# Attention scores as couples of 64-row matmuls, in one stage, without stacking copies

## The chip, the cores and the metric

The kernel runs on one core of a Trainium2 chip. Its engines work side by side: TensorE does the matmuls (PE in the rows; PEld is its weight loader), VectorE (DVE) and ScalarE (ACT) the elementwise work, GpSimd (POOL) a little at the start, and SyncE's queue (SP) issues the DMAs. The metric is the device time of one execution in microseconds (us); lower is better.

## The reference

Attention with a sliding window of 128 positions and 4 sink positions, then a feed-forward layer (FFN). Shapes: `q`, `k`, `v` are [4, 8, 768, 64] (batch, heads, positions, width), `w_in` is [512, 2048], `w_out` [2048, 512], all float32.

```python
scores = np.matmul(q, k.transpose(0, 1, 3, 2)) / np.sqrt(D)
keep = (pos[None, :] < n_sink) | ((rel >= 0) & (rel < window))   # rel = pos[:, None] - pos[None, :]
scores = np.where(keep, scores, -1e9); scores -= scores.max(-1, keepdims=True)
a = np.exp(scores); a /= a.sum(-1, keepdims=True) + 1e-9
x = np.matmul(a, v)                     # [B, H, S, D] -> [B*S, H*D] = [3072, 512]
h = x @ w_in
out = (h * np.clip(h + 3, 0, 6) / 6) @ w_out
```

## The kernel before

A unit is 256 positions (two tiles of 128, called t) of one batch: 4 batches x 3 units make 12 units. Attention is done by pairs of heads: 4 pairs for a unit, 48 in all (list `pus`; the four units at the start of a sequence come first). A head has 64 channels, so one pair fills the 128 partitions with K, Q or V: head 0 in rows 0 to 63, head 1 in rows 64 to 127.

Nearly all matmuls use fp32r operands, split into a rounded high part and the remainder as a low part (`split_parts`, `copy_r`: a copy on ACT, a subtraction on DVE). The first 12 pairs are "plain" (`plain`): their scores are plain fp32 matmuls of 64 rows, straight from the loaded `kr` and `qr` (L334). The other 36 are "split". For them `B_k` and `B_q` make `kt` and `qt` (high, low), and eight SP DMAs stack these into `K` and `Q`, where one head's channels fill all 128 rows: Q high over Q low, K high twice, K low twice. One full-height matmul (L338) with Q as weights then gives two of the four products of parts; two matmuls make the scores of one head and tile. A split pair so has 8 score matmuls, and for the 32 split pairs that are not at the start of a sequence they have 272 columns (128 previous, 128 own, 16 sink positions).

Then for each pair: `C_mask` (DVE, L355: score plus mask, and its minimum), `merge` (DVE L363), `C_exp` (ACT L382), `C_sum` (DVE), `C_norm` (ACT L369), `C_sinks` (the sink columns `ssc`, DVE), `D_pt` (PE transposes, L419 and L421), `D_part` (triangles of the transposed blocks, `pm`, DVE L436), `D_out` (`ph` on ACT, `pl` on DVE), `D_sinks` (`pz`, ACT L459), `E_av` (products with V, PE L495), `E_low`/`E_sum`/`E_split` (`tmp`, `xh`, `xl`). `A_split` splits V.

The FFN of a finished unit is a queue of 32 steps for PE: `ffn1` (12 matmuls of 256 columns into one `hps`, L554) and `ffn2` (6 of 512 columns into an output bank `o`, L581). Two `ffn1` and two `ffn2` alternate. Each finished `hps` posts `activate` (`gf`: ACT, then DVE) one tick later and `split` (`gh`, then `g` on DVE) two ticks later. `drain(1)` emits one step.

From slot 14 on the order of PE, ACT, DVE and SP is written out by hand. One slot handles one pair and runs the 8 stages of `STAGES` (L709); each ends with one drained FFN step, so a slot has 8 steps and a unit's 4 slots its 32. Within a slot `s` the steps speak of three pairs: loads and splits of K and Q for pair s, scores to transposes for pair s-1, products with V for pair s-2. `F` puts the posted work in. Engines work their own instructions in order. PSUM has 8 banks, all one pool (`bank`); a new tile waits until the old one's readers are done. `kt`, `qt`, `K` and `Q` have one buffer each.

Of the kernel before, what the change touches and what calls it, by code (L numbers as in the profile page):

```python
# [9 lines left out]
F32 = mybir.dt.float32  # L10
# [8 lines left out]
P = 128  # L19
# [25 lines left out]
def attn_ffn_kernel(ctx: ExitStack, tc: tile.TileContext, qx, kx, vx, vfx, vsx, n_sink, window, w_in, w_out, out):  # L45
# [210 lines left out]
        if not planned:  # L256
            A_split(s)

    def A_split(s):
        split_parts(nc, *st_[s]["vr"], nc.scalar, nc.vector)  # L260

    def B_k(s, part=None):
        if plain(s):
            return
        w = ncol(pus[s][1])
        d = st_[s]
        if part != 1:
            d["kt"] = work.tile([P, 2, 400], F32R, name="kt", bufs=1)  # L270
            copy_r(nc, nc.scalar, d["kt"][:, 0, 0:w], d["kr"][:, 0:w])
        if part == 0:
            return
        kt = d["kt"]
        nc.vector.tensor_tensor(out=kt[:, 1, 0:w], in0=d["kr"][:, 0:w], in1=kt[:, 0, 0:w].bitcast(F32), op=ALU.subtract)
        K = work.tile([P, 2, 2, 400], F32R, name="K", bufs=1)
        for h in range(2):
            for r in range(2):
                nc.sync.dma_start(out=K[D * r:D * (r + 1), h, :, 0:w].bitcast(F32),
                                  in_=kt[D * h:D * (h + 1), :, 0:w].bitcast(F32))  # L280
        d["K"] = K

    def B_q(s, part=None):
        if plain(s):
            return
        d = st_[s]
# [7 lines left out]
        Q = work.tile([P, 2, UT], F32R, name="Q", bufs=1)  # L294
        for h in range(2):
            for r in range(2):
                nc.sync.dma_start(out=Q[D * r:D * (r + 1), h, :].bitcast(F32),
                                  in_=qt[D * h:D * (h + 1), r, :].bitcast(F32))
        d["Q"] = Q

    def spans(u):
        if u:
# [9 lines left out]
            return st_[s][f"P{h}"][:, t * P + c0:t * P + c1]  # L312
        return st_[s]["P"][:, h, t, c0:c1]

    def C_score(s, h, planned=False):

        b, u, p = pus[s]
        d = st_[s]
        if h == 0:
            d["nb"], d["sm"], d["rc"] = (work.tile([P, 4], F32, name=x, bufs=3) for x in ("nb", "sm", "rc"))  # L320
            if not plain(s):
                d["P"] = work.tile([P, 2, 2, WP], F32, name="Pt", bufs=1)
        elif plain(s):
            return
        heads = range(2) if plain(s) else (h,)
        found = []
        for t, (k0c, w, m) in enumerate(spans(u)):
            ts, ks = slice(t * P, (t + 1) * P), slice(k0c, k0c + w)
            sp = {g: ps.tile([P, 512], F32, tag="bank", name="sp") for g in heads}
            found.append(sp)  # L330
            for g in heads:
                if plain(s):
                    gs = slice(D * g, D * (g + 1))
                    nc.tensor.matmul(out=sp[g][:, 0:w], lhsT=d["qr"][gs, ts], rhs=d["kr"][gs, ks],  # L334
                                     start=True, stop=True)
                else:
                    for part in range(2):
                        nc.tensor.matmul(out=sp[g][:, 0:w], lhsT=d["Q"][:, g, ts], rhs=d["K"][:, g, part, ks],  # L338
                                         start=(part == 0), stop=(part == 1))
            if not planned:  # L340
                C_mask(s, t, sp)
        d[f"sp{h}"] = found
        if u and h == 1 and not planned:
            merge(s)

    def C_mask(s, t, sp):
        b, u, p = pus[s]
        d = st_[s]
        k0c, w, m = spans(u)[t]
        for g in sp:  # L350
# [192 lines left out]
    def ffn1(x, i, pool, psum, half, state, tag):  # L543
# [12 lines left out]
        if half == 1:  # L556
            g = pool.tile([P, 2, UT], F32R, tag="g", name="g", bufs=2)
            gh = pool.tile([P, 2, UT], F32R, tag="gh", name="gh", bufs=2)
            gf = pool.tile([P, 2, UT], F32, tag="gf", name="gf", bufs=2)
            state[i] = (gh, g)  # L560

            def activate():
                nc.scalar.activation(out=gf, in_=hp, func=AF.Relu, bias=three, scale=1.0)  # L563
                nc.vector.scalar_tensor_tensor(out=gf, in0=gf, scalar=6.0, in1=hp, op0=ALU.min, op1=ALU.mult)  # L564

            def split():
                copy_r(nc, eng(GHI, state["n"] * NP), gh, gf)
# [98 lines left out]
                queues.append(ffn_steps(units.index((b, u)), xt[(b, u)], work, ps, ps, dsts, "bank"))  # L666

    FROM = 3 * NP + 2
    ORDER = "V C0 - C1 E0 X - E1 L - N - Bk - Bq W - D0 - D1 -"
    MULT = [1] * 9 + [2] * 3  # L670
    WN = [0, 1, 1, 1, 1, 2, 2, 2, 3, 6, 6, 7]

    for s in range(FROM):
        if s == 3:
            later_constants()
        for step in ORDER.split():
            if step == "-":
                drain(MULT[s] if s < len(MULT) else 1)
            elif step in ("C0", "C1", "X", "N"):
                if 0 <= s - 1 < NS:  # L680
                    if step[0] == "C":
                        C_score(s - 1, int(step[1]))
                    else:
                        {"X": C_exp, "N": C_norm}[step](s - 1)
                    if step == "X" and s - 1 < NP:
                        keep_busy(2 * WARM[2] if s > 1 else WARM[1])
            elif step[0] == "E":
# [18 lines left out]
            elif step[0] == "D" and 0 <= s - 1 < NS:  # L706
                D_pt(s - 1, int(step[1]))

    STAGES = ("v C0 p1 F o1 z", "C1 E0 t0 F", "t1 m F a0 Kh Qh", "E1 F X Kl Ql b0", "c F N", "S F a1 b1 vs", "D0 x F V", "D1 p0 F o0 L")  # L709

    def stage(s, steps):
        c, e = s - 1, s - 2
        for step in steps.split():
            if step == "F":
                run_due()
            elif step in ("v", "Kh", "Kl", "Qh", "Ql", "V", "L", "vs"):
                if step == "L":
                    if s + 1 < NS:
                        A_kq(s + 1)
                elif s < NS and step != "vs":  # L720
                    {"v": lambda: A_v(s, True), "Kh": lambda: B_k(s, 0), "Kl": lambda: B_k(s, 1),
                     "Qh": lambda: B_q(s, 0), "Ql": lambda: B_q(s, 1), "V": lambda: A_split(s)}[step]()
                if c < NS and pus[c][1:] == (1, 0):
                    if step == "v":
                        batch_loads(pus[c][0])
                    elif step == "vs":
                        batch_split()
            elif step in ("C0", "C1", "t0", "t1", "m", "X", "c", "N", "S", "D0", "D1", "p0", "o0"):
                if c < NS:
                    {"C0": lambda: C_score(c, 0, True), "C1": lambda: C_score(c, 1, True),  # L730
                     "t0": lambda: [C_mask(c, t, st_[c]["sp0"][t]) for t in range(2)],
                     "t1": lambda: [C_mask(c, t, st_[c]["sp1"][t]) for t in range(2)],
                     "m": lambda: merge(c) if pus[c][1] else None, "X": lambda: C_exp(c, True), "c": lambda: C_sum(c),
                     "N": lambda: C_norm(c, True), "S": lambda: C_sinks(c), "D0": lambda: D_pt(c, 0, True),
                     "D1": lambda: D_pt(c, 1, True), "p0": lambda: D_part(c, 0), "o0": lambda: D_out(c, 0)}[step]()
            elif step in ("p1", "o1", "z"):
                if s > FROM and e < NS:
                    {"p1": lambda: D_part(e, 1), "o1": lambda: D_out(e, 1), "z": lambda: D_sinks(e)}[step]()
            elif e < NS:
                {"E0": lambda: slot_E(e, 0, True), "E1": lambda: slot_E(e, 1, True), "a0": lambda: E_low(e, 0),  # L740
                 "b0": lambda: E_sum(e, 0), "a1": lambda: E_low(e, 1), "b1": lambda: E_sum(e, 1),
                 "x": lambda: E_split(e)}[step]()

    ET = mybir.EngineType
    with tc.manual_schedule(engines={ET.PE, ET.Activation, ET.DVE, ET.SP}):
# [179 lines left out]
```

## Time and profile before

| | |
|---|---|
| device time, 3 runs | 726.91, 728.89, 730.55 us; median 728.89 |
| the profiled execution | 727.6 us; its span, first to last instruction, 725.7 us |
| PE busy | 708.4 us, 98% of the span |
| PE weight loads | 636.0 us, 88% |
| DVE, ACT busy | 514.6 us (71%), 449.2 us (62%) |
| granted TensorE clock, mean | 0.999 of full speed |

A timeline row gives start and duration in us, engine, line, operation and tiles; several equal instructions are merged in one row (x4), whose duration runs to the end of the last. Matmul durations hold the way through the array, so matmuls overlap in them: what one costs is the distance to the start of the next. In brackets stands how long the engine was idle before, and what ended that.

### The profile page before, as it was taken

What the parts mean: (1) busy time and instruction counts of PE and PEld (TensorE: products, weight loads), DVE (VectorE), ACT (ScalarE), POOL (GpSimd) and SP (SyncE); (2) the same over time, 40 slices, a digit from 0 to 9 for tenths busy, and PEclk for the clock granted to TensorE, in tenths of its full rate; (3) what the DMA queues carried; (4) which work ended last, traced back from release to release, by engine and by line L of the source; (5) the groups of instructions that cost most, each with busy time, mean ns of one, the idle gap of its engine ahead of it and who ended that gap; (6) DMA issues with size and microseconds to landing.
All of it is one profiled execution on the core that took longest, in us unless ns stands there. A gap on an engine that the chain in (4) does not pass through costs nothing.

```text
span 725.7 us, 13651 instructions
## 1 busy us (share of the span) xinstructions
PE 708.4 (98%) x4804; PEld 636.0 (88%) x4804; DVE 514.6 (71%) x1330; ACT 449.2 (62%) x1171; POOL 5.0 (1%) x19
## 2 busy tenths in 40 slices
PE   8999999999999999999999999999999999999996
PEld 7777887899989989988999898999998998899995
DVE  5799996446677778777877786777777877775321
ACT  5999875546447656666666566665756665654322
POOL 2000000000000000000000000000000000000000
PEclk9999999999999999999999999999999999999999
DMA  7667563124444544454345534644454454420000
GB/s 242 190 201 238 184 216 95 45 80 109 128 118 102 135 123 119 113 137 134 103 115 142 131 98 119 150 119 119 120 131 116 120 126 125 127 70 1 30 1 33
DMA packets 53549, 87.23 MB, mean 120 GB/s; under 512 B 8161, under 2 KB 36321, under 8 KB 53473
## 3 DMA queue, kind: packets, MB, share of 16 engines
q1 hardware_dynamic: 53328, 86.28, 43.1%
q8 instruction: 40, 0.66, 0.4%
q14 instruction: 37, 0.30, 0.1%
q10 hardware_dynamic: 144, 0.00, 0.0%
HBM read 42.21 MB, written 6.29 MB: 67 GB/s over the span
## 4 chain that ended last, share of the span: by engine, by line
PE 79%; ACT 10%; DVE 5%; DMA 4%; issue 2%; ACTq 0%; DVEq 0%; SPq 0%
PE hps L554 33%; PE o L581 30%; PE av L495 7%; PE sp L338 5%; PE pt L419 2%; ACT Ph L382 2%; DMA st<-in_w_out_dram 2%; ACT wt L153 1%; ACT Pt L369 1%; ACT st L157 1%; DVE pm L436 1%; ACT ph L35 1%; ACT Ph L369 1%; PE sp L334 1%; ACT pf L35 1%
## 5 line engine op out<-in xcount | busy, mean ns | idle before, releaser
L554 PE MATMUL hps<-xh,wih 128*128 128x256 f32 x768 | 221.1, 288 | 2.0 <-ACT wih L35 1.4
L554 PE MATMUL hps<-xh,wil 128*128 128x256 f32 x768 | 217.1, 283 | 0.0
L554 PE MATMUL hps<-xl,wih 128*128 128x256 f32 x768 | 216.4, 282 | 0.1
L581 PE MATMUL o<-woh,gh 128*128 128x512 f32 x384 | 153.7, 400 | 1.3 <-DVE gh L41 1.3
L581 PE MATMUL o<-woh,g 128*128 128x512 f32 x384 | 152.4, 397 | 0.1
L581 PE MATMUL o<-wol,gh 128*128 128x512 f32 x384 | 151.2, 394 | 0.0
L554 PEld LDWEIGHTS hps<-xh,wih 128*128 128x128 f32 x768 | 144.8, 189 | 4.7 <-ACT wih L35 1.7
L554 PEld LDWEIGHTS hps<-xl,wih 128*128 128x128 f32 x768 | 144.9, 189 | 1.9 <-DVE xl L517 0.3
L554 PEld LDWEIGHTS hps<-xh,wil 128*128 128x128 f32 x768 | 144.7, 188 | 0.8 <-DVE nb L355 0.7
L564 DVE SCALAR_TENSOR_TENSOR gf<-gf,hps 128x512 f32<-128x512 f32 x96 | 65.6, 684 | 72.7 <-ACT gf L563 72.7
L563 ACT ACTIVATE gf<-hps,three 128x512 f32<-128x512 f32 x96 | 65.8, 686 | 76.2 <-PE hps L554 75.9
L35 ACT ACTIVATE ph<-pm 128x512 fp32r<-128x512 f32 x64 | 40.5, 632 | 101.8 <-DVE pm L436 101.8
L581 PEld LDWEIGHTS o<-woh,g 128*128 128x128 f32 x384 | 72.1, 188 | 20.3 <-DVE g L568 3.3
L581 PEld LDWEIGHTS o<-woh,gh 128*128 128x128 f32 x384 | 72.3, 188 | 12.9 <-ACT Ph L369 1.5
L581 PEld LDWEIGHTS o<-wol,gh 128*128 128x128 f32 x384 | 72.5, 189 | 11.2 <-issue 0.3
L382 ACT ACTIVATE Pt<-Pt,nb 128x144 f32<-128x144 f32 (+2 forms) x144 | 58.6, 409 | 35.5 <-DVE Pt L363 31.8
L568 DVE TENSOR_TENSOR g<-gf,gh 128x512 fp32r<-128x512 f32 x96 | 66.2, 690 | 16.8 <-ACT gh L35 14.1
L30 DVE TENSOR_TENSOR pl<-pm,ph 128x512 fp32r<-128x512 f32 x64 | 44.3, 692 | 30.4 <-ACT ph L35 27.9
L338 PE MATMUL sp<-K,Q 128*128 128x272 f32 (+2 forms) x288 | 48.7, 291 | 2.3 <-DMA Q<-qt 1.6
L355 DVE CUSTOM_DVE_ANT_0 Pt<-sp,m_t 128x272 f32<-128x272 f32 x128 | 50.2, 434 | 0.0
L338 PEld LDWEIGHTS sp<-K,Q 128*128 128x128 f32 x288 | 42.7, 188 | 7.5 <-issue 2.0
L35 ACT ACTIVATE gh<-gf 128x512 fp32r<-128x512 f32 x72 | 44.9, 624 | 6.8 <-DVE gf L564 6.8
(99 smaller groups left out, 993.8 us busy)
## 6 DMA issues: line engine op xcount, KB each, us to landing
K<-kt SPq DMA_DIRECT2D x128, 200.0 KB, 3.3
Q<-qt SPq DMA_DIRECT2D x144, 64.0 KB, 2.4
st<-in_w_in_dram SPq DMA_DIRECT2D x16, 512.0 KB, 4.1
st<-in_w_out_dram SPq DMA_DIRECT2D x16, 512.0 KB, 4.7
kr<-in_kx_dram SPq DMA_DIRECT2D x32, 200.0 KB, 2.7
qr<-in_qx_dram SPq DMA_DIRECT2D x48, 128.0 KB, 2.4
out_dram<-ost SPq DMA_DIRECT2D x24, 256.0 KB, 2.2
vr<-in_vx_dram SPq DMA_DIRECT2D x32, 192.0 KB, 2.9
```

What stands on the lines that cost most here:

```text
L30: lo_engine.tensor_tensor(out=lo, in0=src, in1=hi.bitcast(F32), op=ALU.subtract)
L35: nc.scalar.mul(out=out, in_=src, mul=scale)
L338: nc.tensor.matmul(out=sp[g][:, 0:w], lhsT=d["Q"][:, g, ts], rhs=d["K"][:, g, part, ks], start=(part == 0), stop=(part == 1))
L355: d["min"] = nc.vector.tensor_tensor_reduce(out=cell(s, g, t, 0, w), in0=sp[g][:, 0:w], in1=m[:, 0:w], scale=-SCALE, scalar=3.0e38, op0=AL ...
L369: nc.scalar.mul(out=blk, in_=blk, mul=c)
L382: d["exp"] = nc.scalar.activation(out=blk, in_=blk, func=AF.Exp, scale=-1.0, bias=d["nb"][:, i:i + 1], accum_out=d["sm"][:, i:i + 1])
L495: nc.tensor.matmul(out=o, lhsT=l, rhs=r, start=(j == 0 and (h == 0 or not plain(s))), stop=(j == len(seq) - 1 and (h == 1 or not plain(s))))
L554: nc.tensor.matmul(out=hp[:, half, :], lhsT=l, rhs=r, start=(j == 0), stop=(j == n - 1))
L563: nc.scalar.activation(out=gf, in_=hp, func=AF.Relu, bias=three, scale=1.0)
L564: nc.vector.scalar_tensor_tensor(out=gf, in0=gf, scalar=6.0, in1=hp, op0=ALU.min, op1=ALU.mult)
L568: eng(GLO, state["n"] * NP).tensor_tensor(out=g, in0=gf, in1=gh.bitcast(F32), op=ALU.subtract)
L581: nc.tensor.matmul(out=acc, lhsT=l[:, f, ts_], rhs=r[i][:, f, :], start=(i == 0 and f == 0 and j == 0), stop=(i == NFP - 1 and f == 1 and ...
```

## The change

The scores of a split pair are taken straight from `kt` and `qt` by matmuls of 64 rows: for each tile t three products (high-high, low-high, high-low; the product of the two low parts is no longer computed), each as a couple, head 0 in rows 0 to 63 and head 1 in rows 64 to 127, into two banks. `K`, `Q` and their DMAs go. All 12 matmuls of a pair stand in one stage ("C", the second); before, four stood in the first stage and four in the second. Other steps change stage: the products with V of head 0 go from stage 2 to stage 3; the triangles and splits of the transposed blocks (p1, o1) from the next slot's first stage to the last stage; the two halves of V's split (V1, V2) from the stage of the transposes to the next slot's stages 2 and 5; `tmp`, `xh` and `xl` move too. In the third unit of FFN work `gh` goes from DVE to ACT (`GHI`).

```diff
+    def A_split(s, part=None):
+        if "vr" not in st_[s]:
+            return
+        hi, lo, src = st_[s]["vr"]
+        if part != 1:
+            copy_r(nc, nc.scalar, hi, src)
+        if part != 0:
+            nc.vector.tensor_tensor(out=lo, in0=src, in1=hi.bitcast(F32), op=ALU.subtract)
+            del st_[s]["vr"]
...
-        K = work.tile([P, 2, 2, 400], F32R, name="K", bufs=1)
-        for h in range(2):
-            for r in range(2):
-                nc.sync.dma_start(out=K[D * r:D * (r + 1), h, :, 0:w].bitcast(F32),
-                                  in_=kt[D * h:D * (h + 1), :, 0:w].bitcast(F32))
-        d["K"] = K
...
-    def C_score(s, h, planned=False):
+    def C_score(s, planned=False):
...
+            sp = [ps.tile([P, 512], F32, tag="bank", name="sp") for g in range(2)]
+            d["sp"].append(sp)
+            if plain(s):
+                terms = [(d["qr"][:, ts], d["kr"][:, ks])]
+            else:
+                terms = [(d["qt"][:, i, ts], d["kt"][:, j, ks]) for i, j in ((0, 0), (1, 0), (0, 1))]
+            for j, (l, r) in enumerate(terms):
+                for g in range(2):
                     gs = slice(D * g, D * (g + 1))
-                    nc.tensor.matmul(out=sp[g][:, 0:w], lhsT=d["qr"][gs, ts], rhs=d["kr"][gs, ks],
-                                     start=True, stop=True)
-                else:
-                    for part in range(2):
-                        nc.tensor.matmul(out=sp[g][:, 0:w], lhsT=d["Q"][:, g, ts], rhs=d["K"][:, g, part, ks],
-                                         start=(part == 0), stop=(part == 1))
+                    nc.tensor.matmul(out=sp[g][:, 0:w], lhsT=l[gs], rhs=r[gs], start=(j == 0),
+                                     stop=(j == len(terms) - 1))
...
-                copy_r(nc, eng(GHI, state["n"] * NP), gh, gf)
+                copy_r(nc, eng(GHI, state["n"] * NP + 1), gh, gf)
...
-    ORDER = "V C0 - C1 E0 X - E1 L - N - Bk - Bq W - D0 - D1 -"
+    ORDER = "V C - E0 X - E1 L - N - Bk - Bq W - D0 - D1 -"
...
-    STAGES = ("v C0 p1 F o1 z", "C1 E0 t0 F", "t1 m F a0 Kh Qh", "E1 F X Kl Ql b0", "c F N", "S F a1 b1 vs", "D0 x F V", "D1 p0 F o0 L")
+    STAGES = ("b F z", "C F t0 V1", "E0 t1 m F Kh Qh", "E1 F a0 X Kl Ql b0", "c V2 F a1 N b1", "S F x v", "D0 F vs p0 o0",
+              "D1 F p1 o1 L")
```

The code that reads `STAGES` (`stage`) is rewritten to match: p1 and o1 now belong to pair s-1, V1 and V2 too, and t0 and t1 mask both heads of one tile.

How TensorE's order changes in a slot in the middle of the program. Before, at its first two stages (`sp` are the scores, `o` an FFN step, `av` the products with V):

```order
L338 MATMUL sp<-K,Q 128x272 x4
L581 MATMUL o_4376<-woh_132,gh 128x512
L581 MATMUL o_4376<-wol_140,gh 128x512
L581 MATMUL o_4376<-woh_132,g 128x512
L581 MATMUL o_4376<-woh_132,gh 128x512
L581 MATMUL o_4376<-wol_140,gh 128x512
L581 MATMUL o_4376<-woh_132,g 128x512
L338 MATMUL sp<-K,Q 128x272 x4
L495 MATMUL av<-ph,VS 128x256
```

And in the changed kernel, at the same place:

```order
L572 MATMUL o_4281<-woh_132,gh 128x512
L572 MATMUL o_4281<-wol_140,gh 128x512
L572 MATMUL o_4281<-woh_132,g 128x512
L329 MATMUL sp<-kt,qt 128x272 x12
L572 MATMUL o_4297<-woh_132,gh 128x512
L572 MATMUL o_4297<-wol_140,gh 128x512
L572 MATMUL o_4297<-woh_132,g 128x512
L572 MATMUL o_4297<-woh_132,gh 128x512
L572 MATMUL o_4297<-wol_140,gh 128x512
L572 MATMUL o_4297<-woh_132,g 128x512
L486 MATMUL av<-ph,VS 128x256
```

Two groups of four score matmuls, with an FFN step between them and `av` right behind the second, have become one group of twelve, and `av` stands one FFN step behind it.

How VectorE's order changes between the second triangle product of one pair (`pm`) and the masks of the next (`Pt,nb<-sp`). Before:

```order
L436 TENSOR_TENSOR pm<-pt,side 128x512
L564 SCALAR_TENSOR_TENSOR gf<-gf,hps 128x512
L30 TENSOR_TENSOR pl<-pm,ph 128x512
L355 ISA Pt,nb<-sp,m_t_98 128x272
L355 ISA nb 128x1
L355 ISA Pt,nb<-sp,m_t_99 128x272
L355 ISA nb 128x1
L568 TENSOR_TENSOR g<-gf,gh 128x512
L355 ISA Pt,nb<-sp,m_t_98 128x272
```

And in the changed kernel:

```order
L427 TENSOR_TENSOR pm<-pt,side 128x512
L30 TENSOR_TENSOR pl<-pm,ph 128x512
L555 SCALAR_TENSOR_TENSOR gf<-gf,hps 128x512
L559 TENSOR_TENSOR g<-gf,gh 128x512
L346 ISA Pt,nb<-sp,m_t_98 128x272
L346 ISA nb 128x1
L346 ISA Pt,nb<-sp,m_t_98 128x272
L346 ISA nb 128x1
L346 ISA Pt,nb<-sp,m_t_99 128x272
```

`gf` and `g` of the FFN now both stand ahead of the first mask, and `gf` stands behind `pl`.

How ScalarE's order changes between the exponentials (`Pt,sm<-Pt,nb`) and the products with the reciprocal sums (`Pt<-Pt,rc`). Before:

```order
L382 ACTIVATE Pt,sm<-Pt,nb 128x144 x4
L563 ACTIVATE gf<-hps,three 128x512
L369 ACTIVATE Pt<-Pt,rc 128x144 x4
L35 ACTIVATE gh<-gf 128x512
L528 COPY tmp<-av 64x256
```

And in the changed kernel:

```order
L519 COPY tmp<-av 64x256
L373 ACTIVATE Pt,sm<-Pt,nb 128x144 x4
L554 ACTIVATE gf<-hps,three 128x512
L519 COPY tmp<-av 64x256
L360 ACTIVATE Pt<-Pt,rc 128x144 x4
L35 ACTIVATE gh<-gf 128x512
```

The second copy `tmp` has moved from behind these products to ahead of them.

## Rows read from the trace of the kernel before

**Rows 1.** Busy time by stretch: start and end in us, length, then busy us and instructions of PE, PEld, DVE, ACT and POOL, the granted clock, the DMA share and GB/s.

```profile
160.00:400.00 240.00, 238.79 (x1662) 218.04 (x1661) 178.62 (x460) 147.67 (x404) 0.00 (x0) 1.00 0.46 120
400.00:640.00 240.00, 237.35 (x1651) 215.95 (x1650) 183.63 (x467) 151.32 (x410) 0.00 (x0) 1.00 0.47 122
```

**Rows 2.** Waits of PE, then of its weight loader, from 136 to 700 us: who waited for whom, us in total, times, the longest.

```profile
PE sp L338 <- DMA Q<-qt: 1.6, 1, 1.6
PE av L495 <- ACT pz L459: 1.6, 4, 0.4
...
PEld av L495 <- ACT pz L459: 3.4, 9, 0.6
...
PEld sp L338 <- issue: 2.0, 2, 1.8
PEld sp L338 <- PE hps L554: 1.6, 6, 0.5
```

**Rows 3.** Timeline of PE around the two groups of score matmuls of an undisturbed slot.

```profile
255.68 0.28 PE L554 MATMUL hps<-xh,wil 128*128 128x256 f32 x1
255.80 0.67 PE L338 MATMUL sp<-K,Q 128*128 128x272 f32 x4
256.31 0.39 PE L581 MATMUL o<-woh,gh 128*128 128x512 f32 x1
256.54 0.39 PE L581 MATMUL o<-wol,gh 128*128 128x512 f32 x1
...
257.46 0.40 PE L581 MATMUL o<-woh,g 128*128 128x512 f32 x1
...
258.20 0.29 PE L495 MATMUL av<-ph,VS 128*128 128x256 f32 x1
```

**Rows 4.** Timeline of PE at three disturbed places; in each, the four score matmuls stand between the two rows.

```profile
445.10 0.29 PE L554 MATMUL hps<-xh,wil 128*128 128x256 f32 x1
...
446.43 0.44 PE L495 MATMUL av<-ph,VS 128*128 128x256 f32 x2 [0.40 <-ACT pz L459]
...
458.24 0.28 PE L554 MATMUL hps<-xh,wil 128*128 128x256 f32 x1
...
459.15 0.39 PE L581 MATMUL o<-woh,gh 128*128 128x512 f32 x1
...
631.36 0.29 PE L554 MATMUL hps<-xh,wil 128*128 128x256 f32 x1
...
633.85 0.39 PE L581 MATMUL o<-woh,gh 128*128 128x512 f32 x1
```

**Rows 5.** Timeline of PE around groups of 64-row matmuls of plain pairs. In fp32 each matmul of the code shows as two, one behind the other. The first group is both heads' matmul of 256 columns, the second one head's alone, the third both heads' of 128 columns.

```profile
54.60 0.28 PE L554 MATMUL hps<-xl,wih 128*128 128x256 f32 x1
54.81 0.70 PE L334 MATMUL sp<-kr,qr 64*128 64x256 f32 x4
...
55.67 0.28 PE L554 MATMUL hps<-xh,wih 128*128 128x256 f32 x1
...
83.91 0.40 PE L581 MATMUL o<-wol,gh 128*128 128x512 f32 x1
84.23 0.70 PE L334 MATMUL sp<-kr,qr 64*128 64x256 f32 x2
...
85.19 0.39 PE L581 MATMUL o<-woh,gh 128*128 128x512 f32 x1
...
108.19 0.28 PE L554 MATMUL hps<-xh,wil 128*128 128x256 f32 x1
108.40 0.49 PE L334 MATMUL sp<-kr,qr 64*128 64x128 f32 x4
...
109.16 0.39 PE L581 MATMUL o<-wol,gh 128*128 128x512 f32 x1
```

**Rows 6.** Timeline of ACT, of DVE and, in the last row, of PE through the slot of rows 3, up to the next pair's first `pm`.

```profile
264.01 0.69 ACT L563 ACTIVATE gf<-hps,three 128x512 f32<-128x512 f32 x1 [0.65 <-PE hps L554]
264.60 1.32 ACT L369 ACTIVATE Pt<-Pt,rc 128x144 f32<-128x144 f32 x4
266.46 0.36 ACT L528 COPY tmp<-av 64x256 f32<-64x256 f32 x1
...
256.71 0.68 DVE L436 TENSOR_TENSOR pm<-pt,side 128x512 f32<-128x512 f32 x1
...
258.70 0.43 DVE L355 CUSTOM_DVE_ANT_0 Pt<-sp,m_t 128x272 f32<-128x272 f32 x1
...
260.87 0.69 DVE L363 TENSOR_TENSOR Pt<-Pt 128x512 f32<-128x512 f32 x1
...
264.73 0.69 DVE L564 SCALAR_TENSOR_TENSOR gf<-gf,hps 128x512 f32<-128x512 f32 x1 [0.95 <-ACT gf L563]
...
266.47 0.69 DVE L568 TENSOR_TENSOR g<-gf,gh 128x512 fp32r<-128x512 f32 x1
...
267.66 0.29 DVE L41 CAST xh<-tmp 128x256 fp32r<-128x256 f32 x1
...
268.33 0.55 DVE L30 TENSOR_TENSOR VS<-vr,VS 128x384 fp32r<-128x384 f32 x1
268.91 0.69 DVE L436 TENSOR_TENSOR pm<-pt,side 128x512 f32<-128x512 f32 x1
...
266.53 0.38 PE L419 MATMUL pt<-ident_r,Pt 128*128 128x128 f32 x2
```

More of the change, by code (lines that the diff above doesn't have):

```diff
@@ L293, in B_q @@
         nc.vector.tensor_tensor(out=qt[:, 1, :], in0=d["qr"], in1=qt[:, 0, :].bitcast(F32), op=ALU.subtract)
[L294 to L299, printed above, removed]
     def spans(u):
@@ L313, in cell @@
         return st_[s]["P"][:, h, t, c0:c1]
-    def C_score(s, h, planned=False):
+    def C_score(s, planned=False):
         b, u, p = pus[s]
         d = st_[s]
[L319 to L326, printed above, removed]
+        d["nb"], d["sm"], d["rc"] = (work.tile([P, 4], F32, name=x, bufs=3) for x in ("nb", "sm", "rc"))
+        if not plain(s):
+            d["P"] = work.tile([P, 2, 2, WP], F32, name="Pt", bufs=1)
+        d["sp"] = []
@@ L327, in C_score @@
         for t, (k0c, w, m) in enumerate(spans(u)):
             ts, ks = slice(t * P, (t + 1) * P), slice(k0c, k0c + w)
[L329 to L332, printed above, removed]
-                    gs = slice(D * g, D * (g + 1))
-                    nc.tensor.matmul(out=sp[g][:, 0:w], lhsT=d["qr"][gs, ts], rhs=d["kr"][gs, ks],
-                                     start=True, stop=True)
-                else:
-                    for part in range(2):
-                        nc.tensor.matmul(out=sp[g][:, 0:w], lhsT=d["Q"][:, g, ts], rhs=d["K"][:, g, part, ks],
-                                         start=(part == 0), stop=(part == 1))
+            sp = [ps.tile([P, 512], F32, tag="bank", name="sp") for g in range(2)]
@@ L340, in C_score, with C_mask @@
             if not planned:
-                C_mask(s, t, sp)
-        d[f"sp{h}"] = found
-        if u and h == 1 and not planned:
+                C_mask(s, t)
+        if u and not planned:
             merge(s)
-    def C_mask(s, t, sp):
+    def C_mask(s, t):
         b, u, p = pus[s]
         d = st_[s]
+        sp = d["sp"][t]
         k0c, w, m = spans(u)[t]
-        for g in sp:
+        for g in range(2):
             i = 2 * g + t
@@ L678, in attn_ffn_kernel @@
                 drain(MULT[s] if s < len(MULT) else 1)
-            elif step in ("C0", "C1", "X", "N"):
+            elif step in ("C", "X", "N"):
                 if 0 <= s - 1 < NS:
[L681 to L684, printed above, removed]
+                    {"C": C_score, "X": C_exp, "N": C_norm}[step](s - 1)
                     if step == "X" and s - 1 < NP:
@@ L715, in stage @@
                 run_due()
[L716 to L722, printed above, removed]
-                if c < NS and pus[c][1:] == (1, 0):
[L724 to L728, printed above, removed]
-                if c < NS:
[L730 to L738, printed above, removed]
@@ new lines, in stage @@
+            elif step == "L":
+                if k + 1 < NS:
+                    A_kq(k + 1)
+            elif step == "z":
+                if s > FROM and e < NS:
+                    D_sinks(e)
+            elif step in ("b", "vs"):
+                if c < NS and pus[c][1:] == (1, 0):
+                    batch_loads(pus[c][0]) if step == "b" else batch_split()
+            elif step in ahead:
+                if k < NS:
+                    ahead[step]()
+            elif step in now:
+                if c < NS:
+                    now[step]()
@@ L739, in stage @@
             elif e < NS:
-                {"E0": lambda: slot_E(e, 0, True), "E1": lambda: slot_E(e, 1, True), "a0": lambda: E_low(e, 0),
-                 "b0": lambda: E_sum(e, 0), "a1": lambda: E_low(e, 1), "b1": lambda: E_sum(e, 1),
-                 "x": lambda: E_split(e)}[step]()
+                behind[step]()
     ET = mybir.EngineType
```

15 lines of the change are left out of this document (12 added, 3 removed).

## The prediction

> **What bounds the kernel now.** First the table of stretches. From 160 to 640 us, where all but a few of the pairs changed here are worked, TensorE (PE) is busy 476.1 of 480 us, at the full granted clock; DVE is busy 75%, ACT 62% [rows 1]. So what TensorE executes is the time: a term that lengthens its work lengthens the run, and one that shortens ACT, DVE or the DMAs shows only where TensorE waits for it. Then the waits: behind the 3.9 us of idle time stand few causes, nearly all at the score matmuls and at the products with V right behind them [rows 2]. Then the timeline, for what a group of score matmuls costs in TensorE's stream, undisturbed [rows 3] and disturbed [rows 4], and what a group of 64-row matmuls costs [rows 5]. Last the slot on ACT and DVE, for how much room they have [rows 6].
>
> **The score matmuls that go.** A group of four stands between FFN matmuls. From the FFN matmul ahead of it to the first behind it pass 0.63 us (255.68 to 256.31); without it 0.12 would (255.68 to 255.80). So it costs 0.51. The second: 0.74 (257.46 to 258.20) less 0.23 for the FFN matmul of 512 columns (256.31 to 256.54), again 0.51 [rows 3]. A pair pays 1.02 us. One matmul takes 0.127 (255.80 to 256.31 for four).
>
> **The score matmuls that come.** Twelve matmuls of 64 rows, in six couples. Whether a couple takes the time of one matmul or of two decides the case, and the plain pairs show it. Both heads' 256 columns: 54.60 to 55.67 is 1.07, less two FFN matmuls of 0.12, leaves 0.83. One head's alone: 83.91 to 85.19 is 1.28, less two of 0.23, leaves 0.82. So the second head is free. Both heads' 128 columns: 108.19 to 109.16 is 0.97, less 0.12 and 0.23, leaves 0.62 [rows 5]. The difference of 0.21 is two passes of 128 columns, 0.105 each; the group of two such passes then has 0.62 - 0.21 = 0.41 us that belong to no column. This is the price of going to 64 rows and back: before the group 0.21 pass from the last FFN matmul to the first row of the couple (54.60 to 54.81), where a normal one follows after 0.12, and behind it the weights of the first full-height matmul load in the open.
>
> The Trainium skill (TensorEngine Tiling (Array Packing), Key Properties) says the engine drains when the tiling mode changes, though not for another tile of the same mode. This speaks against the change; the trace agrees, with the 0.41 us just read. By that page's speed-up of up to two (Theoretical Speedup) without the drain, a pair would cost 6 x 0.127 = 0.76, not 1.02, and the run would end a further 12 us below my forecast.
>
> No row shows couples in fp32r. From below, 272 columns at the FFN's rate, (0.23 - 0.12) / 256 = 0.43 ns a column, are 0.117 us; from above, the 0.127 of today's matmul with the same columns (two one after the other is a rival below). I take 0.122. A pair's group costs 0.41 + 6 x 0.122 = 1.14 (1.11 to 1.17), 0.12 more than now. Times 32 pairs: +3.8 us (+2.9 to +4.8). The four split pairs at the start of a sequence have 128 and 256 columns: eight matmuls at about 0.12 now, 0.41 + 3 x 0.105 + 3 x 0.12 = 1.09 then, together +0.5. Sum **+4.3 us**. So one matmul time in four is saved, and the change of mode eats all of it.
>
> **The waits that go.** (a) The products with V wait for `pz`. Where it is long, 445.10 to 446.43 is 1.33 against 0.63 undisturbed: 0.70 lost; four of these [rows 2, 3, 4]: 2.8 us. Five shorter ones: the loader's nine waits sum to 3.4; less four of 0.57, 1.1 remain, and each shows a weight load of about 0.1 besides: 1.6. (b) Scores wait for a bank of `hps`: 458.24 to 459.15 is 0.91 against 0.63, 0.28 lost; seven, one of them longer by 0.2 [rows 2, 4]: 2.2. (c) One waits for the DMA of `Q`: 631.36 to 633.85, 2.49 against 0.63: 1.9. (d) Another short one: 0.2. Sum **8.7 us**.
>
> Do they go? (c) must, the DMAs are gone. (a): `pz` is made by p1, o1, z behind the transposes. Between these and the products with V stood two FFN steps and two score groups, now three steps and the group: one step more, 6 x 0.23 = 1.4 us, and p1 stands a stage earlier. The longest wait was 0.6. (b): the changed group opens with a bank of an older `hps`, and TensorE empties before couples anyway. From above all 8.7 go; from below half of them come back in another place. I take 8.7, and 1.0 us for small new ones (a group's middle couples now need both `pm` of the pair before; the copy to `kt` on ACT now waits for the group's end, with the exponentials queued behind it, and these wait for DVE's masks longer than that).
>
> **The rest.** 288 DMAs go (eight a split pair) and the rows put no other wait of TensorE on them: 0. `gh` of one unit moves from DVE to ACT, both idle over 20% there: 0. V's split has a whole slot until it is used: 0. The first 140 us keep their order but for two pairs' splits: 0, give or take 1.
>
> **Sum.** 727.6 (the profiled execution: its span of 725.7 and 1.9 around it) + 4.3 - 8.7 + 1.0 = 724.2 us. The median shown, 728.9, is 1.3 above the profiled one, which lies inside the three runs' spread (726.9 to 730.6); I lean a little towards it and say **724.7**.
>
> **Rivals.**
> *Couples of fp32r run one after the other.* Against: the fp32 couples [rows 5]. For: no row shows fp32r in 64 rows. Then a group costs 0.41 + 12 x 0.122 = 1.87, 0.85 over now, 27 us for 32 pairs and 3 for the four (0.41 + 6 x 0.105 + 6 x 0.12 = 1.76 against 0.96, four times): 727.6 + 30 - 8.7 + 1 = **750**, slower. It decides from the second matmul of a couple costing over 0.06.
> *ACT and DVE become the bound.* Their work forms a ring: the exponentials, `gf`, the products, `gh`, `g`, `xh`, two `pm` with `ph`, the masks, and the next exponentials. Its slack now is the 0.65 us that ACT idles before `gf` for TensorE [rows 6]. New in it: `tmp` ahead of the products, 0.36. From the second `pm` to `merge` pass 4.16 now (256.71 to 260.87). Then `ph`, `gf`, `gf`, `gh` and `g` follow each other before the masks: five steps at about 0.66 (ACT to DVE 0.72, 264.01 to 264.73; ACT to ACT 0.59, 264.01 to 264.60), `g` 0.6, four masks 1.6 (258.70 to 260.87 less `g`): 5.5, so +1.3. Out of it: V's low half 0.58 (268.33 to 268.91) and the wait of `xh` for the second `tmp`, 0.58 (266.47 to 267.66 less 0.61). Together +0.5 to +0.6: the slack shrinks to about 0.1. A late ring does not stop TensorE at once: the transposes at 266.53 come 1.3 us after the two products they need (264.60 + 2 x 0.305), 0.9 with `tmp` ahead, and one slot in four has no `gf` there and catches up. If the ring is 0.6 longer than I add, three slots lag 1.8, 0.9 over the room, in eight units: 7 us, **731**.
> *The waits move.* Half of the 8.7 return, at the middle couples or elsewhere: 727.6 + 4.3 - 4.3 + 1 = **728.6**.
>
> **How the numbers follow.** Forecast 0.62 (own range 720.5 to 728), serial couples 0.08, ring 0.15, waits that move 0.15. A measurement of this kernel tells about 0.5% from no change, 3.6 us: faster is below 725.2, slower above 732.5. The forecast lies across the first bound: 0.72 of it below. Faster 0.45; the same 0.17 + 0.15 + 0.08 = 0.40; slower 0.08 and about half of the ring's, 0.15. The range goes from 719.5 (couples at 0.117, no new wait, 1 us gained at the start: 720.8, and 1 for the prices of the waits) to 734 (the ring with its lag doubled lies above).
>
> **What would show it.** Right: the distance across a group of twelve between 1.2 and 1.3 us behind a matmul of 256 columns, the members of a couple starting within 0.02 us, no wait for `Q` or `pz`, waits of PE and its loader at `sp` and `av` under 2 us. Wrong: twelve starts 0.12 apart (serial); ACT no longer idle before `gf` and TensorE waiting at the transposes (ring); a DVE wait inside the group (waits moved).

## The result and the profile after

The changed kernel takes 733.76 us (median of 7 runs, 733.23 to 735.47); the kernel before, on the same chip, 726.91 (7 runs, 726.11 to 730.55). The ratio is 1.0088, its 95% interval 1.0067 to 1.0108: slower by about 0.9%. Forecast were 724.7 us and a gain. The profiled execution took 733.43 us, and its span is 731.7; before, they were 727.6 and 725.7. So the trace has to account for +6.0 us of span, where the prediction's sum gave -3.4 (724.2 - 727.6).

The stretches first, columns as in [rows 1]:

```profile
160.00:400.00 240.00, 236.98 (x1697) 209.16 (x1696) 170.16 (x446) 150.76 (x407) 0.00 (x0) 1.00 0.14 45
400.00:640.00 240.00, 236.79 (x1702) 209.10 (x1701) 178.10 (x459) 148.98 (x400) 0.00 (x0) 1.00 0.15 49
```

TensorE was idle 3.9 us of these 480 before and is 6.2 us now; the DMA share fell from 0.46 to 0.14. What it waits for, from 136 to 700 us, columns as in [rows 2]:

```profile
PE o L572 <- ACT gh L35: 6.2, 8, 0.8
...
PEld sp L329 <- issue: 9.3, 26, 0.4
PEld o L572 <- ACT gh L35: 7.8, 8, 1.0
PEld pt L410 <- ACT Pt L360: 4.4, 26, 0.2
PEld o L572 <- DVE g L559: 3.8, 9, 0.4
```

The last row has a forerunner in the kernel before, which [rows 2] leave out:

```profile
PEld o L581 <- DVE g L568: 2.8, 9, 0.4
```

All waits of [rows 2] for `Q`, `pz` and `hps` are gone. A new one stands in their place, eight times and each time long: an FFN matmul `o` waits for `gh` from ACT. (The loader's 9.3 us at `sp` are the opening of the new score groups and belong to their price, below.)

The score group, to set beside [rows 3] (TensorE's timeline):

```profile
551.46 0.39 PE L572 MATMUL o<-woh,g 128*128 128x512 f32 x1
551.78 1.01 PE L329 MATMUL sp<-kt,qt 64*128 64x272 f32 x12
552.73 0.50 PE L572 MATMUL o<-woh,gh 128*128 128x512 f32 x1
553.06 0.39 PE L572 MATMUL o<-wol,gh 128*128 128x512 f32 x1
```

From 551.46 to 553.06 pass 1.60 us, less two FFN matmuls of 0.23: 1.14, as forecast.

The new wait stands at the end of each unit. The slot of [rows 6] is itself a unit's last, and two rows of the same timelines that it leaves out are, on ACT and then on TensorE:

```profile
265.82 0.62 ACT L35 ACTIVATE gh<-gf 128x512 fp32r<-128x512 f32 x1
...
266.67 0.48 PE L581 MATMUL o<-woh,gh 128*128 128x512 f32 x1
```

The same place in the changed kernel (in a later unit), TensorE and ACT:

```profile
558.35 0.39 PE L572 MATMUL o<-woh,gh 128*128 128x512 f32 x1
...
561.13 0.53 PE L410 MATMUL pt<-ident_r,Pt 128*128 128x128 f32 x2
562.46 0.50 PE L572 MATMUL o<-woh,gh 128*128 128x512 f32 x1 [0.80 <-ACT gh L35]
...
557.12 0.37 ACT L519 COPY tmp<-av 64x256 f32<-64x256 f32 x1 [1.24 <-PE av L486]
557.72 0.42 ACT L373 ACTIVATE Pt<-Pt,nb 128x144 f32<-128x144 f32 x1 [0.22 <-DVE Pt L354]
...
559.45 0.69 ACT L554 ACTIVATE gf<-hps,three 128x512 f32<-128x512 f32 x1
560.16 0.36 ACT L519 COPY tmp<-av 64x256 f32<-64x256 f32 x1
560.55 1.33 ACT L360 ACTIVATE Pt<-Pt,rc 128x144 f32<-128x144 f32 x4
561.79 0.61 ACT L35 ACTIVATE gh<-gf 128x512 fp32r<-128x512 f32 x1
```

Behind a unit's last hidden block (the last `hps`) TensorE has two `ffn2` steps of 1.4 us each and the transposes; then it needs that block's `gh`. In the other slots steps of the next `ffn1` lie between, at a unit's end none. Before, `gh` ended at 266.44 (265.82 + 0.62) and was used at 266.67: the room was 0.2 us, a number the trace of before held ready and the prediction didn't read. The loader's nine waits for `g` in that trace stand at the same place, behind `gh`, one at each unit's end: there was no room there even then. Now `gf` starts late, ACT no longer idles for it (before, 0.65), `tmp` stands ahead of the products, and `gh` behind both. From the transposes to the FFN matmul behind them pass 0.14 us before (266.53 to 266.67) and 1.33 now (561.13 to 562.46). The wait comes once a unit, in eight units; the distance is 1.32 to 1.36 in seven of them and 1.00 in the first.

### The profile page after: what moved, and what is told of

Its sections match the earlier page's. It is cut to its first block, busy times and chain, and to the rows that moved or that the text cites. A ratio compares the mean times of both kernels' runs of the same rounds, so it can differ in the third digit from the quotient of the medians.

```text
span 731.7 us, 13157 instructions
## 1 busy us (share of the span) xinstructions
PE 712.6 (97%) x4948; PEld 625.0 (85%) x4948; DVE 505.6 (69%) x1322; ACT 454.7 (62%) x1179; POOL 5.0 (1%) x19
## 4 chain that ended last, share of the span: by engine, by line
PE 54%; ACT 23%; DVE 16%; issue 3%; DMA 3%; ACTq 0%; DVEq 0%; SPq 0%
PE hps L545 22%; PE o L572 22%; ACT Pt L373 5%; PE av L486 4%; ACT Pt L360 4%; PE sp L329 4%; ACT gh L35 3%; DVE g L559 3%; DVE Pt L346 3%; DVE pl L30 3%; DVE pm L427 3%; ACT ph L35 2%; ACT Ph L373 2%; DMA st<-in_w_out_dram 2%; ACT gf L554 2%
## 5 line engine op out<-in xcount | busy, mean ns | idle before, releaser
L572 PE MATMUL o<-woh,gh 128*128 128x512 f32 x384 | 156.5, 408 | 7.5 <-ACT gh L35 6.2
L35 ACT ACTIVATE gh<-gf 128x512 fp32r<-128x512 f32 x80 | 50.0, 625 | 21.6 <-DVE gf L555 21.3
L519 ACT COPY tmp<-av 64x256 f32<-64x256 f32 x72 | 26.5, 368 | 47.7 <-PE av L486 46.8
L360 ACT ACTIVATE Pt<-Pt,rc 128x144 f32<-128x144 f32 (+2 forms) x144 | 48.7, 409 | 1.4 <-DVE rc L381 0.5
L346 DVE CUSTOM_DVE_ANT_0 Pt<-sp,m_t 128x272 f32<-128x272 f32 x128 | 48.6, 435 | 1.2 <-PE sp L329 1.2
```

The lines of the kernel that those rows point to most:

```text
L35: nc.scalar.mul(out=out, in_=src, mul=scale)
L360: nc.scalar.mul(out=blk, in_=blk, mul=c)
L572: nc.tensor.matmul(out=acc, lhsT=l[:, f, ts_], rhs=r[i][:, f, :], start=(i == 0 and f == 0 and j == 0), stop=(i == NFP - 1 and f == 1 and ...
```

## The experiments

Each run is timed against the kernel before on the same chip. The runs form four groups, e1 to e4, e5 to e8, e9 to e12 and e13 with e14; the median of the kernel before was 727.6, 727.8, 726.8 and 726.4 in them, so a difference between runs of different groups, and any difference from the changed kernel's 733.76, is good to about 1 us. Edits are shown against the changed kernel unless said otherwise. Three theories stood at the start: ACT and DVE's ring got too long where `g` moved ahead of the masks (A); `tmp` ahead of the products makes `gh` late (B); the couples cost more than their rows show (C). From e5 on the expectations use the letters anew: A says that the loss is the one wait for `gh` at a unit's end, and B is the rival that each names, mostly that the ring holds back the whole unit.

**e1, masks first.** The first two masks ahead of the FFN step's `gf` and `g`.

```diff
-"C F t0 V1"
+"C t0 F V1"
```

> The changed kernel with one edit: in the second stage the masks of the first tile stand ahead of the FFN's posted work (C t0 F V1). Theory A, the ring of ACT and DVE is the bound: DVE no longer idles 0.7 us for gh ahead of the masks, so the ring falls from 14.43 us to about 13.7, under TensorE's 14.25. The FFN's gf in the last slot of a unit then starts when its hps is done, not 0.95 us later, and TensorE's wait for gh there (1.08 us, eight times) goes but for 0.2: 1.2 to 1.4 us a unit, 10 in all, 724 us (0.3 to 0.5% under before). Theory B, the second copy tmp ahead of the products is the cause: it still stands there, the wait stays, 732 to 734. Theory C, the couples themselves cost more than the stream shows: 733.

731.63 us (729.96 to 733.08), ratio 1.0054 (1.0036 to 1.0073). This is better than the changed kernel by 2.1, and far from A's 724. From the transposes to `o` at a unit's end:

```profile
558.80 0.38 PE L410 MATMUL pt<-ident_r,Pt 128*128 128x128 f32 x2
559.82 0.51 PE L572 MATMUL o<-woh,gh 128*128 128x512 f32 x1 [0.64 <-ACT gh L35]
```

The distance is 1.02 in place of 1.33: the ring was a part of it, no more.

**e2, the copy behind.** The second `tmp` behind the products, as in the kernel before.

```diff
-"c V2 F a1 N b1", "S F x v"
+"c V2 F N", "S F a1 b1 x v"
```

> The changed kernel with one edit: the second tmp and its sum go back behind the products and the sinks (c V2 F N; S F a1 b1 x v). Theory B: gh comes 0.39 us earlier in every slot, the wait at a unit's end shrinks from 1.08 to 0.7, 8 x 0.4 = 3 us, 730.5. Theory A: 0.39 is taken out of the ring and 0.5 to 0.6 put in, since xh now waits for that sum: the ring stays at 14.4 to 14.6, gh gains 0.39 in its slot and loses 0.1 to 0.2 in each of three, so 733 to 735, no gain. Theory C: 733.8.

730.93 us (729.95 to 731.67), ratio 1.0045 (1.0029 to 1.0060), as B had it. The same place:

```profile
558.06 0.38 PE L410 MATMUL pt<-ident_r,Pt 128*128 128x128 f32 x2
558.89 0.50 PE L572 MATMUL o<-woh,gh 128*128 128x512 f32 x1 [0.45 <-ACT gh L35]
```

The distance is 0.83. The copy costs 0.5 us a unit, and more than half of the delay is something else.

**e3, the couples alone.** The twelve matmuls and no DMAs, but every other step in the stage it had before (the code that reads the new step names is left out here).

```diff
-"b F z", "C F t0 V1", "E0 t1 m F Kh Qh", "E1 F a0 X Kl Ql b0", "c V2 F a1 N b1", "S F x v", "D0 F vs p0 o0", "D1 F p1 o1 L"
+"v b P1 F O1 z", "C E0 t0 F", "t1 m F a0 Kh Qh", "E1 F X Kl Ql b0", "c F N", "S F a1 b1 vs", "D0 x F V", "D1 p0 F o0 L"
...
```

> The couples without the other moves: all twelve score matmuls in the second stage, and every other step in the stage it had before. Theory A: the ring is that of before, with 0.65 us of slack; the group costs 0.1 us a pair more than the two groups did (+4), the waits for the DMA of Q and for the bank of hps go (-4), those for pz may stay: 726 to 728.5, and no wait for gh at the unit's end over 0.3. Theory C: 731 to 734 as with the whole change.

728.67 us (727.85 to 730.10), ratio 1.0015 (1.0003 to 1.0028). Its waits:

```profile
PE av L486 <- ACT pz L450: 1.1, 4, 0.3
...
PEld av L486 <- ACT pz L450: 3.0, 9, 0.5
```

The waits for `pz` are back, those for `Q`, `hps` and `gh` are not there. The time is 0.2 us above A's range and 2 below C's, so C falls: the couples, less the two kinds of waits that they take away, cost 1 us against before.

**e4, the stages alone.** The changed kernel's stages, with `K`, `Q`, their DMAs and eight full-height matmuls in the second stage.

```diff
-            for j, (l, r) in enumerate(terms):
-                for g in range(2):
...
+                    for part in range(2):
+                        nc.tensor.matmul(out=sp[g][:, 0:w], lhsT=d["Q"][:, g, ts], rhs=d["K"][:, g, part, ks],
+                                         start=(part == 0), stop=(part == 1))
```

> The stages of the changed kernel with the scores of before: stacked K and Q by DMA, eight full-height matmuls, all in the second stage. Theory A: the ring is that of the changed kernel and holds the slots at 14.4; TensorE's stream is 0.1 us a pair shorter, which shows only where it does not wait for the ring, so 730 to 734, with the wait for gh at the unit's end still there, 1.0 us or more, eight times. Theory C: the couples are gone, so 726 or less.

731.97 us (731.52 to 734.16), ratio 1.0060 (1.0043 to 1.0076), and the same wait:

```profile
PE o L584 <- ACT gh L35: 6.2, 8, 0.8
```

It met A's range, and the loss lies in the moved steps. A cheaper score group (1.00 in place of 1.14, below) gains little while ACT sets the unit's end.

**e5, both orders.** e1 and e2 together.

> The edits of e1 and e2 together: masks ahead of the FFN step, and the second products' sums behind the sinks, so that ACT's copy of `av` no longer stands ahead of the products. At each unit's end TensorE waited for `gh` 1.08 us in the changed kernel, 0.86 in e1, 0.67 in e2. Theory A (that one wait is the loss; both edits shorten the same chain from the masks by `gf`, copy and products to `gh`): each gain adds to the other, 0.22 + 0.41, the wait is 0.45 and the median 729 (728 to 730). Theory B (ACT and DVE's ring bounds the whole unit, and a wait that goes comes back at the transposes): 731, like each of them alone. If the products' sums come too late for the next scores' banks, or the two edits undo each other: above 732.

726.57 us (726.02 to 727.75), ratio 0.9980 (0.9966 to 0.9995): 7.2 below the changed kernel. From the transposes to `o` pass 0.50:

```profile
555.91 0.38 PE L410 MATMUL pt<-ident_r,Pt 128*128 128x128 f32 x2
556.41 0.50 PE L572 MATMUL o<-woh,gh 128*128 128x512 f32 x1
```

In the rows the two gains add up (0.31 + 0.50, and 0.83 together). In the times they come to more than the two alone (2.1 + 2.8 = 4.9), but by 2.3 us, which the intervals of the four ratios do not clear. The run ended below the range that either theory gave. ACT's timeline in this kernel shows a further cause, one that neither edit touches:

```profile
551.92 0.37 ACT L519 COPY tmp<-av 64x256 f32<-64x256 f32 x1 [1.38 <-PE av L486]
552.19 0.42 ACT L373 ACTIVATE Pt<-Pt,nb 128x144 f32<-128x144 f32 x1
...
553.92 0.69 ACT L554 ACTIVATE gf<-hps,three 128x512 f32<-128x512 f32 x1
```

The masks are done here (`merge` starts at 550.88), yet the exponentials begin at 552.19, 1.31 behind it and right behind head 0's `tmp`, which has waited for TensorE's `av`; in the changed kernel they come 0.79 behind `merge` (556.93 to 557.72), because there the masks end later than this `tmp`. The change moved `av` a stage later, and its `tmp` with it, to the place in front of the exponentials. So faster masks alone do not make `gf` early. No run moved this copy alone.

**e6, `gh` on DVE.** The last block's rounding on the engine where no products stand ahead.

```diff
-                copy_r(nc, eng(GHI, state["n"] * NP + 1), gh, gf)
+                copy_r(nc, nc.vector if i == NFP - 1 else eng(GHI, state["n"] * NP + 1), gh, gf)
```

> The changed kernel, with only the rounding of a unit's last hidden block (`gh` of the eighth FFN step) on DVE, where it is not queued behind the copy of `av` and the products on ACT. Theory A (the loss is the wait for `gh` at a unit's end, 1.08 us in eight units): `gh` follows DVE's `gf` at once, 0.43 long, some 0.9 us earlier; the wait falls to 0.1 to 0.3, eight times 0.8 to 0.95 is gained: 726.5 (725.5 to 728), a span of 724 to 725.5. Theory B (the ring bounds the unit; TensorE then waits for the same chain at the next place, the transposes or the next unit's products): 731 to 734, and new waits at `pt` in the unit's last slot. In between, 728 to 731, a part of the wait goes to `g`, which follows `gh` on DVE.

737.67 us (736.63 to 738.90), ratio 1.0132 (1.0107 to 1.0157): 3.9 slower than the changed kernel, a miss for both theories. DVE's timeline shows why:

```profile
562.00 0.68 DVE L555 SCALAR_TENSOR_TENSOR gf<-gf,hps 128x512 f32<-128x512 f32 x1
...
563.72 0.20 DVE L41 CAST ssc<-Pt 128x64 fp32r<-128x64 f32 x1 [0.58 <-ACT Pt L360]
...
564.10 0.42 DVE L41 CAST gh<-gf 128x512 fp32r<-128x512 f32 x1
```

`gf` was ready at 562.68, but the instruction kept its place in the program, and on DVE that is behind `ssc`, which itself waits for ACT's products. `gh` ends at 564.52 and TensorE starts at 564.57, 1.62 behind the transposes (562.95).

**e7**, e5 with e6's edit:

> e5 and e6 together. Theory A: with the wait at the unit's end gone nothing is left to win, TensorE's own work sets the time: like e6, 726 (725 to 727.5); the couples alone (e3), which have the same matmuls and no such wait, took 728.7 with 4 us of other waits. Theory B: the ring still lags in the regular slots (14.4 us from merge to merge against TensorE's 14.25) and only e1's and e2's edits make it shorter: more than 2 us below e6.

729.33 us (728.80 to 731.33), ratio 1.0029 (1.0012 to 1.0045), 2.8 above e5, for the same reason. **e8**, e7 with the stacking DMAs and eight full-height matmuls in one group:

> e7, but with the stacking DMAs and the eight full-height score matmuls in one group, as in e4. Tells what the couples of 64 rows cost when no wait covers it. By the traces a group of twelve costs 1.17 us in TensorE's stream and one group of eight 0.98; 36 such pairs: 6.8 us. If TensorE's work bounds e7 and e8 alike (theory A): 719 (717.5 to 721), below both kernels. If the ring bounds (theory B), or the DMAs to `K` and `Q` are waited for again: not below e7 by more than 2 us. If the couples are as cheap as one group (the price read from the trace is covered by something else): equal to e7.

724.09 us (723.03 to 726.19), ratio 0.9943 (0.9923 to 0.9964): 5.2 below e7, with nearly the same wait of TensorE for `gh` in both (3.3 and 3.2 us in all). The couples cost that much against one full-height group.

**e9, `gh` early.** As e6, but posted with `gf`, so that it stands right behind it, and `g` behind it in turn.

```diff
-            post(2, split)
+            post(1 if i == NFP - 1 else 2, split)
```

> The changed kernel, with the rounding of a unit's last hidden block on DVE and, other than in e6, right behind DVE's `gf`, ahead of `tmp` and `ssc` (in e6 it stood behind `ssc`, which waits for the products on ACT, and the wait for `gh` grew from 1.08 to 1.38 us). Theory A (the loss of the changed kernel is the wait for `gh` at a unit's end, because `gh` stands behind the products in its queue): the wait falls under 0.15, eight times 1.0 us go, 725.8 (725 to 727.5). Theory B (`tmp`, `ssc` and with them `xh`, `pz` come 1.1 us later in that slot and TensorE waits for these in place of `gh`): 729 or more, with waits at `hps` or `av` in the slot behind.

726.85 us (726.12 to 729.16), ratio 0.9997 (0.9982 to 1.0012): 6.9 below the changed kernel, inside theory A's range. At a unit's end, TensorE, then ACT and DVE:

```profile
556.92 0.53 PE L410 MATMUL pt<-ident_r,Pt 128*128 128x128 f32 x2
557.20 0.48 PE L572 MATMUL o<-woh,gh 128*128 128x512 f32 x1
...
555.24 0.69 ACT L554 ACTIVATE gf<-hps,three 128x512 f32<-128x512 f32 x1
...
555.99 0.68 DVE L555 SCALAR_TENSOR_TENSOR gf<-gf,hps 128x512 f32<-128x512 f32 x1
556.71 0.43 DVE L41 CAST gh<-gf 128x512 fp32r<-128x512 f32 x1
```

The distance is 0.28 in place of 1.33, with `gf` as late as in the changed kernel and `tmp` still ahead of the products. Eight times 1.05 are 8.4 us, of which the time shows 6.9. The rounding of one block a unit, put elsewhere with its remainder `g`, takes back the loss. The ring is still late, as the loader's short waits at the transposes show, which e9 shares with the changed kernel:

```profile
PEld pt L410 <- ACT Pt L360: 4.2, 25, 0.2
```

**e10**, e5 with that edit (timed in the same group as e9):

> e5 with the same early rounding. e5 has 0.33 us of waiting for `gh` left in each of eight units. Theory A: 2.6 us less than e5: 724 (723.3 to 725.5). Theory B: not below e5's 726.6.

723.17 us (722.17 to 725.11), ratio 0.9938 (0.9916 to 0.9961): 3.7 below e9, and the waits at `pt` are gone. **e11**, e8 with it, so with stacked copies:

> e8 (stacking DMAs and eight full-height score matmuls in one group, with e5's orders) with the early rounding. e8 has 0.63 us of waiting left in each of eight units. Theory A: 5.0 us less: 719 (718 to 720.5), the fastest of all, and about 5 us under e10, which is the price of the couples when nothing hides it. Theory B: 722 or more.

717.89 us (717.12 to 718.58), ratio 0.9867 (0.9841 to 0.9893): the fastest of all, 5.3 below e10. Its score group:

```profile
538.59 0.40 PE L584 MATMUL o<-woh,g 128*128 128x512 f32 x1
538.82 1.16 PE L341 MATMUL sp<-K,Q 128*128 128x272 f32 x8
539.82 0.39 PE L584 MATMUL o<-woh,gh 128*128 128x512 f32 x1
```

538.59 to 539.82 is 1.23, less 0.23: 1.00 against 1.14 for the twelve; 0.14 times 36 pairs are 5.0.

**e12**, meant to part the twelve into two groups:

> e10, with the couples of the two halves of the rows in two groups of six matmuls, an FFN step between them: the change to 64 rows and back is paid twice a pair. If the 0.41 us read from the plain pairs belongs to each change of mode, 32 to 36 pairs pay 13 to 15 us more than e10: 738 (736 to 740). If most of a group's price is something else, as the first wait for a bank, under 8 us more.

723.64 us (722.88 to 727.06), like e10: the edit, with `C1` behind `F` in the second stage, did not part them. `F` puts in only ACT's and DVE's posted work, and TensorE's FFN matmuls come at the end of a stage, so the twelve stayed side by side:

```profile
530.21 1.01 PE L332 MATMUL sp<-kt,qt 64*128 64x272 f32 x12
```

**e13** parts them for real, the second half a stage later (against e10; `C0` and `C1` are the two halves of `C`):

```diff
-"C t0 F V1", "E0 t1 m F Kh Qh"
+"C0 t0 F V1", "C1 E0 t1 m F Kh Qh"
...
```

> e10, with the couples of the second half of the rows in the next stage, so that matmuls of an FFN step stand between two groups of six (in e12 none stood there). If 0.41 us belong to each change of mode, 32 to 36 pairs pay 13 to 15 us more than e10's 723.2: 737 (735 to 739), and a group of six costs 0.41 + 3 x 0.122 = 0.78 in TensorE's stream. If a group's price beyond its couples is smaller than read, say 0.2: 730. Above 740, if the second half's masks, which come a step later, make TensorE wait besides.

736.89 us (735.82 to 739.04), ratio 1.0150 (1.0133 to 1.0166): 13.7 more than e10.

```profile
642.14 0.39 PE L575 MATMUL o<-woh,g 128*128 128x512 f32 x1
642.46 0.65 PE L332 MATMUL sp<-kt,qt 64*128 64x272 f32 x6
643.03 0.50 PE L575 MATMUL o<-woh,gh 128*128 128x512 f32 x1
643.38 0.39 PE L575 MATMUL o<-wol,gh 128*128 128x512 f32 x1
```

642.14 to 643.38 is 1.24, less 0.46: 0.78 for a group of six. Two of these less one group of twelve (1.14) leave 0.42 for one change to 64 rows and back; 32 to 36 pairs make 13.4 to 15.1 us, and the time shows 13.7. The Trainium skill (TensorEngine Tiling (Array Packing), Key Properties) says that TensorE drains at a change of mode; the row agrees and gives the price.

**e14**, e10 with three matmuls of head 0, then three of head 1, for each half:

```diff
-            for j, (l, r) in enumerate(terms):
-                for g in range(2):
+            for g in range(2):
+                for j, (l, r) in enumerate(terms):
```

> e10, with each half's six matmuls as three of head 0, then three of head 1, in place of couples. If matmuls on different halves of the rows run beside each other only when they follow each other directly in the stream, only the third and the fourth of each six do: the group then costs 0.41 + 10 x 0.122 = 1.63 in place of 1.17, 16 us more for 36 pairs: 739 (736 to 742). If both halves work off their own matmuls, however these are ordered: like e10, 723 (722 to 725). If couples never overlap: like e10 as well, but then a group would last 1.87, which the traces of all kernels with couples speak against.

722.95 us (722.04 to 725.47), ratio 0.9952 (0.9936 to 0.9968), like e10, and so is the group:

```profile
544.51 1.02 PE L329 MATMUL sp<-kt,qt 64*128 64x272 f32 x12
```

The two heads' matmuls run beside each other although they don't stand next to each other in the program.

## Why the prediction was wrong, point by point

- **TensorE bounds the kernel**: right; it is busy 97% of the span after, and what was lost shows where it waits.
- **The score groups**: right to the digit. Twelve cost 1.14 us, the change of mode 0.42 (0.41 forecast), and a couple one matmul's time, 0.12; the members of a couple start within 0.01 us of each other in the trace, as the sign asked. The rival of serial couples is out.
- **The waits that go**: right, none of the three kinds is left. **New small waits**, 1.0: there are such, the loader's short ones at `pt` and at `g` among them, but more of them (next point).
- **These terms together**: they held where the ring keeps up. e10, which has neither the stall at the units' ends nor the late ring, is 3.6 us under the kernel before (723.17 against 726.81), where the sum said 3.4. e9, where the stall is gone and the ring as late as in the changed kernel, equals the kernel before (726.85). So the late ring costs another 3.7 us outside the stall, where the sum had 1.0 for all small waits.
- **The range**: its lower end, 720.8 less 1, does not quite come out of the terms given for it (724.2 less 0.9, 1 and 1 is 721.3); nothing rests on this. That 733.8 still lies just inside the range is luck: its upper end was set for a late ring that stops TensorE at the transposes, not for this stall.
- **The step that failed** is the judgement that ACT and DVE keep a slack of about 0.1 us and that TensorE therefore does not wait for them. The rival that they become the bound got 0.15, and it happened. It was priced at 731, and the run took 733.8. Three things in it were wrong.
 - *Where TensorE stops.* "A late ring does not stop TensorE at once: the transposes at 266.53 come 1.3 us after the two products they need." The transposes have most of that room (the loader waits there 0.2 us at most), but at a unit's end `gh` had 0.2 us, and it stands behind the products in ACT's queue. The slot of [rows 6], from which the slack was read, is such a unit's end, and the waits for `g` were in the same answer as [rows 2]. With 0.2 of room the copy ahead of the products (0.36) already had to show there, ring or no ring. The other slots have no such consumer, and all of them were counted alike. e9 shows it: with `gh` out of that queue TensorE's wait goes, though the rest stays late.
 - *How much longer the ring is.* "Together +0.5 to +0.6". It is measured on these rows of the changed kernel, DVE and ACT:

```profile
551.39 0.68 DVE L427 TENSOR_TENSOR pm<-pt,side 128x512 f32<-128x512 f32 x1
...
556.93 0.69 DVE L354 TENSOR_TENSOR Pt<-Pt 128x512 f32<-128x512 f32 x1
...
549.40 0.69 DVE L427 TENSOR_TENSOR pm<-pt,side 128x512 f32<-128x512 f32 x1
...
545.01 0.69 ACT L554 ACTIVATE gf<-hps,three 128x512 f32<-128x512 f32 x1
```

 Second `pm` to `merge` is 5.54, the 5.5 forecast. But from `gf` to the first `pm` it is 4.39 against 4.90 (264.01 to 268.91 in [rows 6]): 0.51 less, where the sum had 0.36 added and 1.16 taken out, 0.80 less. The copy delays the products by 0.5, not 0.36, and some 0.1 less falls away behind `g`. The ring grew by 1.38 - 0.51 = 0.87. That is over the 0.65 it had, and it fell behind TensorE.
 - *A second way to be late.* The order on ACT, which the section on the change shows, puts head 0's `tmp` ahead of the exponentials. That this copy waits for a product with V that had moved a stage later was not followed up. In e5, where the masks are early, it is what the exponentials follow, and ACT does not idle before `gf`. In the changed kernel it comes into play in a unit's first two slots; in the last two the masks end later still.
- The edits measure the parts at a unit's end, in us from the transposes to `o`: 1.33; 1.02 without the longer way to the masks (e1); 0.83 without the copy (e2); 0.50 without both (e5); 0.28 with `gh` off that queue (e9).
- The signs listed beforehand told the case apart: no ACT idle time before `gf` was there. "TensorE waiting at the transposes" named the smaller part: the loader's short waits at `pt` are 0.2 us at most, and the long ones stand one matmul further on.

What stays open: e9's wait is gone by 8.4 us in the rows and its time by 6.9, known to about 1. Of the rows' 8.4, 7.6 show between the first and the last of the loader's nine waits for `g`: 485.3 us in the changed kernel (136.66 to 621.96) and 477.7 in e9 (138.14 to 615.81). e9's later start belongs to its profiled execution (728.14, over the median of 726.85), whose granted clock was 0.96 from 100 to 140 us, against 1.00. Where the remaining 0.8 went was not separated, nor how the 3.7 us between e9 and e10 divide among the late masks, the copy and the waits at the transposes.

## What to carry to other kernels

When steps are moved between stages, find for each queue that they pass the consumer with the least room, at the rare places too (the end of a unit, the first and the last slot), and compare each added delay with that room rather than with the mean slack. Here an engine at 62% busy set the time through the order of its queue alone, and moving an instruction to another engine helped only when nothing ahead of it there waited for the late work (e6 and e9). When a change bundles a new form of a computation with a new order of the work, time them apart: here the order, once mended, was worth about 9 us (e11 against before) with the old form of the scores in one group, and the new form cost 5 against that (e10 against e11).

## What the runs showed of the hardware beyond the forecast

- One change to 64-row matmuls and back costs 0.42 us of TensorE's time (e13: the same twelve matmuls take 1.14 in one group and twice 0.78 in two).
- Matmuls on the two halves of the rows overlap also where three of one half precede three of the other (e14: 1.02 for twelve, as in couples).
- The rounding of 128x512 to fp32r took 0.43 us on DVE (e9) and 0.61 on ACT (the changed kernel).
- e11 moves 87.23 MB by DMA and e10 49.43, and e11 is the faster: no wait of TensorE or its loader for the stacking copies shows in its trace from 136 to 700 us.
